# Softmax logits with the eight keys of a row innermost, in a two-layer-type network on one core

## The chip, the cores and the metric

The kernel runs on one core of a Trainium2 chip. A core has a matrix engine (TensorE, "PE" in the profile), a vector engine (VectorE, "DVE"), a scalar engine (ScalarE, "ACT"), a general engine (GpSimd, "POOL") and a queue that starts transfers (SyncE, "SP"). Each takes its own instructions in order and waits on semaphores for the others. The working memory, SBUF, and the memory that TensorE writes, PSUM, both have 128 partitions; a shape such as 128x1280 means 1280 numbers of float32 in each partition. The metric is the time of one execution on the device in microseconds; several executions are summarised by their median.

## The reference

A sequence of 2048 rows of 640 numbers passes through four layers, each added to its input after a normalisation of the rows: local attention, a Fourier mixing, local attention, the same mixing.

```python
def _A_ref(x, wqkv, wo):              # H = 32 heads of Dh = 20; W, dil = 8, 2
    q, k, v = (x @ wqkv) split by head
    idx = pos[:, None] - (arange(W) * dil)[None, :]      # 8 keys a row, every second row back
    logits = einsum("bhsd,bhswd->bhsw", q, kg) * scale   # kg, vg gathered by idx
    logits = where(idx >= 0, logits, -1e9)
    attn = softmax(logits, axis=-1)                      # over the 8 keys
    o = einsum("bhsw,bhswd->bhsd", attn, vg)
    return o.reshape(B, S, D) @ wo
def _B_ref(x, dft_seq_re, dft_seq_im, dft_hid_re, dft_hid_im):
    a, b = x @ dft_hid_re.T, x @ dft_hid_im.T
    return dft_seq_re @ a - dft_seq_im @ b
x = x + _A_ref(layernorm(x), wqkv, wo); x = x + _B_ref(layernorm(x), ...)
x = x + _A_ref(layernorm(x), wqkv, wo); x = x + _B_ref(layernorm(x), ...)
```

## The kernel before, in words

The rows are dealt to 4 chunks (`NC`) of 128 partitions with 4 rows each (`NJ`). The 32 heads are cut into 8 groups of 4 (`NE`, `HE`). One group of one chunk is a *unit* `u` of attention, 32 units in a layer; a unit is worked off in two halves (`jp`), each with two rows a partition: 2 rows x 8 keys x 4 heads x 20 = 1280 products. A half is a *step* `s = 2u + jp`; steps run from about -7 to 66. Functions are put into a plan by `at(step, phase, function)`, and the list `PHASES` sets the order of phases within a step. In the attention layers the order of all five engines is exactly this written order. In the mixing layers (`LayerB`) only TensorE's order is written; the other engines' instructions there are ordered by the compiler's planner.

For one unit the engines do this:

- SyncE loads windows of keys and values (`w_load`, L420) and the queries (`q_load`); ScalarE copies the queries into PSUM (`q_copy`, L407), in the phase `qc` late in the step ahead.
- VectorE multiplies the queries by the keys (`qk_mul`, L434, 1280 products into one of four tiles `pr`). GpSimd adds the second ten of a head's 20 products to the first ten (L437), so that `qk_red` on VectorE (L444) sums 10 numbers a logit. In the steps listed in `WHOLE` (one list for each attention layer) GpSimd is left out and VectorE sums all 20.
- The logits of a unit, `lg`, lie in SBUF as row, key, head: 128 numbers a partition. The softmax on VectorE has six parts (`soft`): the mask (L459, in chunks that hold the beginning of the sequence), the maximum over the keys (L461), its subtraction (L463), the sum (L465), the reciprocal (L467) and the product (L469), which writes the probabilities `pp` to PSUM. Between L463 and L465 ScalarE takes the exponential (L452). The maximum and the sum run over the keys, which lie 4 numbers apart, because the 4 heads are innermost.
- `av_mul` (L474) multiplies the probabilities, each repeated over 20 numbers, by the values, and `av_tree` on GpSimd adds the 8 keys in three additions (L493, L494, L495). The last half of a layer is summed on VectorE instead (L490).

Beside this TensorE computes the projections to queries, keys and values (L365, evacuated by ScalarE at L372), transposes (L330, and L338 for the low halves, with copies by ScalarE at L334 and L353), the output projection (L518, added to the row by VectorE at L162, with the row statistics by ScalarE at L167, L169 and GpSimd at L177) and, as fill towards the end of a layer, the first products of the mixing layer (L976, with splits at L910 and L963). ScalarE is in order too: the exponential and the copy of the queries stand in its queue among the evacuations that TensorE waits for. TensorE's float32 products are made of three passes over high and low halves.

The first attention layer runs from about 40 to 390 us of the span, the second from about 870 to 1260. The tile `pq` is one bank of PSUM: the queries `qp`, the probabilities `pp`, the maximum `mx`, the sum `sm` and the mask `mk`.

## Time and profile before

| | |
|---|---|
| median of the runs | 1773.27 us (1769.95 to 1776.17, 3 runs) |
| the profiled execution | 1771.33 us, of which the span on the engines is 1769.3 us |
| TensorE busy | 1736.0 us (98%) |
| VectorE busy | 1388.5 us (78%) |
| ScalarE busy | 810.8 us (46%) |
| GpSimd busy | 624.6 us (35%) |
| mean granted clock of TensorE | 0.995 |

The profile is one execution. Rows of groups give line, engine, operation, the tiles written and read, the shapes, the count, then the busy time, the mean duration in ns, and the idle time ahead of them with what ended it. Rows of waits give who waited, for whom, the time in total, how often and the longest. Rows of stretches give the window, its length, and busy time (with instruction count) of TensorE, its weight loads ("PEld"), VectorE, ScalarE and GpSimd, then the granted clock, the share of the transfer engines, and GB/s. Rows in order of time give start and duration in us; a bracket is the idle time just before and its releaser. TensorE's instructions overlap, so its busy time is the union of their spans, and short stalls may hide in it.

### The profile page before, as it was taken

What the parts mean: (1) busy time and instruction counts of PE and PEld (TensorE: products, weight loads), DVE (VectorE), ACT (ScalarE), POOL (GpSimd) and SP (SyncE); (2) the same over time, 40 slices, a digit from 0 to 9 for tenths busy, and PEclk for the clock granted to TensorE, in tenths of its full rate; (3) what the DMA queues carried; (4) which work ended last, traced back from release to release, by engine and by line L of the source; (5) the groups of instructions that cost most, each with busy time, mean ns of one, the idle gap of its engine ahead of it and who ended that gap; (6) DMA issues with size and microseconds to landing.
All of it is one profiled execution on the core that took longest, in us unless ns stands there. A gap on an engine that the chain in (4) does not pass through costs nothing.

```text
span 1769.3 us, 26448 instructions
## 1 busy us (share of the span) xinstructions
PE 1736.0 (98%) x8798; PEld 1505.9 (85%) x8798; DVE 1388.5 (78%) x2127; ACT 810.8 (46%) x1686; POOL 624.6 (35%) x587
## 2 busy tenths in 40 slices
PE   9999998989999999999999999999999999999999
PEld 6889897878888888888898889988788888888888
DVE  5999999977767767767548999999777676686673
ACT  4654544554445445445534344444434443443441
POOL 3899988850000000000028998899200000000000
PEclk9999999999999999999999999999999999999999
DMA  7996769858777787786657866698688767867761
GB/s 269 309 325 212 220 202 311 274 170 277 274 254 232 243 269 232 246 270 222 206 185 223 264 213 219 202 334 275 203 283 290 247 211 243 260 218 239 255 203 53
DMA packets 270760, 426.19 MB, mean 241 GB/s; under 512 B 22528, under 2 KB 149504, under 8 KB 270368
## 3 DMA queue, kind: packets, MB, share of 16 engines
q1 hardware_dynamic: 267424, 422.54, 72.3%
q10 hardware_dynamic: 3200, 1.97, 0.4%
q8 instruction: 70, 1.15, 0.3%
q14 instruction: 66, 0.54, 0.1%
HBM read 339.28 MB, written 85.14 MB: 240 GB/s over the span
## 4 chain that ended last, share of the span: by engine, by line
PE 59%; DVE 20%; DMA 9%; POOL 5%; issue 4%; ACT 3%; SPq 0%; DVEq 0%; ACTq 0%; POOLq 0%
PE aux L1058 13%; PE t L1147 11%; PE m L1147 11%; PE m L365 9%; PE pq L1147 5%; PE xt L1147 5%; DVE pr L434 4%; DVE pr L474 3%; DMA xc<-stg 3%; PE aux L518 3%; DVE lg L444 2%; POOL pr L493 2%; DMA win<-kvb 1%; POOL pr L437 1%; DVE stg L1111 1%
## 5 line engine op out<-in xcount | busy, mean ns | idle before, releaser
L365 PE MATMUL m<-r,s 128*128 128x480 f32 x1920 | 436.2, 381 | 2.7 <-ACT r L129 2.2
L365 PEld LDWEIGHTS m<-r,s 128*128 128x128 f32 x1920 | 355.4, 188 | 56.3 <-ACT r L129 2.7
L1058 PE MATMUL aux<-r2a,zo 128*128 128x320 f32 x768 | 226.5, 310 | 0.0
L1140 ACT CAST r<-win 128x512 fp32r<-128x512 f32 x246 | 150.5, 620 | 158.4 <-DVE win L1176 75.4
L493 POOL TENSOR_TENSOR pr<-pr 128x640 f32<-128x640 f32 x126 | 208.2, 1652 | 37.3 <-DVE pr L474 36.7
L1058 PE MATMUL aux<-pr,zo 128*128 128x320 f32 x704 | 208.3, 308 | 0.0
L177 POOL TENSOR_TENSOR stats<-stats,mhalf 128x1 f32<-128x1 f32 (+1 forms) x40 | 29.0, 726 | 493.8 <-ACT stats L173 484.7
L1141 DVE TENSOR_TENSOR r<-win,r 128x512 fp32r<-128x512 f32 x246 | 166.3, 688 | 45.0 <-ACT r L1140 43.8
L434 DVE TENSOR_TENSOR pr<-pq,win 128x1280 f32<-128x1280 f32 x128 | 189.7, 1483 | 9.7 <-ACT stg L372 4.8
L474 DVE TENSOR_TENSOR pr<-pq,win 128x1280 f32<-128x1280 f32 x128 | 190.7, 1491 | 4.9
L437 POOL TENSOR_TENSOR pr<-pr 128x640 f32<-128x640 f32 x118 | 168.8, 1431 | 16.2 <-DVE pr L434 15.7
L1147 PE MATMUL m<-r,r 128*128 128x512 f32 x594 | 152.6, 392 | 0.0
L1058 PEld LDWEIGHTS aux<-r2a,zo 128*128 128x128 f32 x768 | 144.1, 188 | 2.0
L1147 PE MATMUL t<-r,r 128*128 128x512 f32 x498 | 135.1, 393 | 1.7 <-PE t L1147 1.7
L1058 PEld LDWEIGHTS aux<-pr,zo 128*128 128x128 f32 x704 | 132.2, 188 | 2.1
L1147 PEld LDWEIGHTS m<-r,r 128*128 128x128 f32 x594 | 111.4, 188 | 24.7
L976 PE MATMUL m<-s,r 128*128 128x512 f32 x384 | 119.8, 400 | 4.0 <-DVE zo L1038 1.5
L976 PE MATMUL t<-s,r 128*128 128x512 f32 x384 | 118.2, 395 | 0.3 <-DVE ot L1033 0.3
L494 POOL TENSOR_TENSOR pr<-pr 128x320 f32<-128x320 f32 x126 | 111.8, 887 | 9.9
L444 DVE TENSOR_REDUCE lg<-pr 128x64 f32<-128x640 f32 (+1 forms) x128 | 110.5, 863 | 4.7 <-POOL pr L437 4.6
L1147 PEld LDWEIGHTS t<-r,r 128*128 128x128 f32 x498 | 93.4, 188 | 23.7 <-PE t L1147 2.5
L372 ACT COPY stg<-m 128x480 f32<-128x480 f32 x128 | 70.9, 554 | 69.5 <-PE m L365 50.2
(290 smaller groups left out, 3233.1 us busy)
## 6 DMA issues: line engine op xcount, KB each, us to landing
win<-cs_in SPq DMA_DIRECT2D x351, 256.0 KB, 4.3
r<-xc SPq DMA_DIRECT2D x240, 256.0 KB, 4.3
win<-kvb SPq DMA_DIRECT2D x96, 440.0 KB, 5.6
xa<-cs_in SPq DMA_DIRECT2D x121, 256.0 KB, 3.9
win<-kvb SPq DMA_DIRECT2D x64, 360.0 KB, 4.5
xc<-stg SPq DMA_DIRECT2D x40, 512.0 KB, 4.2
kvb<-stg SPq DMA_DIRECT2D x60, 320.0 KB, 5.3
s<-c0b SPq DMA_DIRECT2D x26, 512.0 KB, 6.1
```

The source lines that it names most:

```text
L365: nc.tensor.matmul(mt[g][:, : 3 * F], st[:, a, k], wq[q][:, b, k], start=n == 0, stop=n == 14)
L434: nc.vector.tensor_tensor(pr, q, wview(u, jp, 0, [[1, FE]]), op=ALU.mult)
L437: nc.gpsimd.tensor_tensor(pv[:, :, 0:10], pv[:, :, 0:10], pv[:, :, 10:20], op=ALU.add)
L444: nc.vector.tensor_reduce(lgs[u][:, 2 * jp : 2 * jp + 2].rearrange("p j w h -> p (j w h)"), prq.pop((u, jp)), axis=AX.X, op=ALU.add,)
L474: nc.vector.tensor_tensor(pr.rearrange("p j w (h d) -> p j w h d", d=DH), lgs[u][:, 2 * jp : 2 * jp + 2].unsqueeze(4).to_broadcast([P, 2, ...
L493: g.tensor_tensor(pr[:, :, 0:4], pr[:, :, 0:4], pr[:, :, 4:8], op=ALU.add)
L494: g.tensor_tensor(pr[:, :, 0:2], pr[:, :, 0:2], pr[:, :, 2:4], op=ALU.add)
L976: self.last = nc.tensor.matmul(self.z[t][k], self.xn[c][:, a, j, k * P : (k + 1) * P], self.ct[s][:, b], start=s == 0 and i == 0, stop=s = ...
L1058: self.last = nc.tensor.matmul(self.ym[e][:, :320], zt[(k, a, ri)][:, j2 * P : (j2 + 1) * P], w[:, e * 320 : (e + 1) * 320], start=(k, a, ...
L1140: nc.scalar.copy(hi, raw)
L1141: nc.vector.tensor_tensor(lo, raw, hi.bitcast(F32), op=ALU.subtract)
L1147: nc.tensor.matmul(bank, w(a, kb), hl[b], start=start and (a, b) == (0, 0), stop=stop and (a, b) == (1, 0),)
```

## The change

The logits `lg` and the probabilities `pp` are laid out as head, row, key, so that the 8 keys of a head and row are adjacent; the maxima and sums are laid out as head, row. The reduction of the query products (`qk_red`) reads its tile in the same order as before and writes each result to its new place; the value product (`av_mul`) reads the probabilities through a view that gives the old order. The maximum and the sum now reduce a contiguous run. The number of instructions and the elements of each stay the same there. Step 63, the last query product of a layer, joins both lists in `WHOLE`: GpSimd's addition L437 goes, and VectorE's L444 sums 1280 numbers instead of 640 in this step.

```diff
-WHOLE = ((43, 45, 47, 49, 51, 55, 57, 59), (51, 57))
+WHOLE = ((43, 45, 47, 49, 51, 55, 57, 59, 63), (51, 57, 63))
...
-            prq[(u, jp)] = pv
+            prq[(u, jp)] = pv.rearrange("p (a h) d -> p a h d", h=HE)
 
         def qk_red(u, jp):
             if jp == 0:
-                lgs[u] = T([P, NJ, W, HE], "lg", bufs=2)
+                lgs[u] = T([P, HE, NJ, W], "lg", bufs=2)
             nc.vector.tensor_reduce(
-                lgs[u][:, 2 * jp : 2 * jp + 2].rearrange("p j w h -> p (j w h)"),
+                lgs[u][:, :, 2 * jp : 2 * jp + 2].rearrange("p h j w -> p (j w) h"),
                 prq.pop((u, jp)),
...
             if part == 0 and (u // NE) % 2 == 0:
-                mw = bass.AP(tensor=mk.tensor, offset=mk.offset, ap=[mk.ap[0], [1, NJ], [1, W], [0, HE]])
+                mw = bass.AP(tensor=mk.tensor, offset=mk.offset, ap=[mk.ap[0], [0, HE], [1, NJ], [1, W]])
...
             if part == 1:
-                v.tensor_reduce(mx, lg.rearrange("p j w h -> p j h w"), axis=AX.X, op=ALU.max)
+                v.tensor_reduce(mx, lg, axis=AX.X, op=ALU.max)
             if part == 2:
-                v.tensor_tensor(lg, lg, mx.unsqueeze(2).to_broadcast([P, NJ, W, HE]), op=ALU.subtract)
+                v.tensor_tensor(lg, lg, mx.unsqueeze(3).to_broadcast([P, HE, NJ, W]), op=ALU.subtract)
             if part == 3:
-                v.tensor_reduce(sm, lg.rearrange("p j w h -> p j h w"), axis=AX.X, op=ALU.add)
+                v.tensor_reduce(sm, lg, axis=AX.X, op=ALU.add)
...
             if part == 5:
-                v.tensor_tensor(pp, lg, sm.unsqueeze(2).to_broadcast([P, NJ, W, HE]), op=ALU.mult)
+                v.tensor_tensor(pp, lg, sm.unsqueeze(3).to_broadcast([P, HE, NJ, W]), op=ALU.mult)
...
-                lgs[u][:, 2 * jp : 2 * jp + 2].unsqueeze(4).to_broadcast([P, 2, W, HE, DH]),
+                lgs[u][:, :, 2 * jp : 2 * jp + 2].rearrange("p h j w -> p j w h").unsqueeze(4).to_broadcast([P, 2, W, HE, DH]),
...
-        pp = pq[:, NJ * FE : NJ * FE + NJ * W * HE].rearrange("p (j w h) -> p j w h", j=NJ, w=W)
+        pp = pq[:, NJ * FE : NJ * FE + NJ * W * HE].rearrange("p (h j w) -> p h j w", j=NJ, w=W)
...
-        mx = pq[:, o : o + NJ * HE].rearrange("p (j h) -> p j h", j=NJ)
-        sm = pq[:, o + NJ * HE : o + 2 * NJ * HE].rearrange("p (j h) -> p j h", j=NJ)
+        mx = pq[:, o : o + NJ * HE].rearrange("p (h j) -> p h j", j=NJ)
+        sm = pq[:, o + NJ * HE : o + 2 * NJ * HE].rearrange("p (h j) -> p h j", j=NJ)
```

## The prediction

> **What bounds the kernel now.** I read the page's totals first, then busy time by stretch, then who waited for whom, then the chain of waits.
>
> ```profile
> span 1769.3 us, 26448 instructions
> PE 1736.0 (98%) x8798; PEld 1505.9 (85%) x8798; DVE 1388.5 (78%) x2127; ACT 810.8 (46%) x1686; POOL 624.6 (35%) x587
> ...
> DVE  5999999977767767767548999999777676686673
> ```
>
> TensorE is idle for 33.3 us of the span (1769.3 - 1736.0); nothing that this change touches can win more than that and what the clock loses around the gaps. The row of digits (tenths busy in 40 slices of 44 us) shows where VectorE is full: slices 2 to 8 and 23 to 28, the two attention layers. In these stretches (columns: length, then busy us of PE, PEld, DVE, ACT, POOL, then granted clock):
>
> ```profile
> 53.00:272.00 219.00, 218.03 (x1130) 193.21 (x1129) 211.26 (x292) 117.54 (x297) 202.89 (x189) 1.00 0.78 249
> 272.00:300.00 28.00, 21.51 (x107) 17.54 (x106) 27.25 (x38) 11.16 (x32) 22.04 (x23) 0.92 0.94 329
> 300.00:372.00 72.00, 66.88 (x353) 58.10 (x351) 66.78 (x98) 36.01 (x85) 65.36 (x60) 0.97 0.75 256
> 1072.00:1160.00 88.00, 88.00 (x481) 79.72 (x479) 82.25 (x123) 40.58 (x102) 76.96 (x72) 1.00 0.70 222
> 1160.00:1249.00 89.00, 82.94 (x434) 71.42 (x432) 83.63 (x121) 40.84 (x104) 81.88 (x76) 0.98 0.85 295
> ```
>
> TensorE's idle time inside attention lies at the ends of the layers: 6.5 us (28 - 21.51) and 5.1 us (72 - 66.88) in the first, 6.1 us (89 - 82.94) in the second. What ends it, and what ScalarE waits for from 53 to 350:
>
> ```profile
> PE aux L338 <- ACT s L334: 3.9, 1, 3.9
> PE aux L330 <- POOL zo L495: 2.8, 1, 2.8
> PE t L338 <- ACT r L334: 2.3, 1, 2.3
> PE pq L330 <- POOL zo L495: 1.7, 1, 1.7
> ...
> ACT lg L452 <- DVE lg L463: 74.8, 28, 6.2
> ACT pq L407 <- DVE pr L474: 27.4, 14, 4.7
> ACT stg L372 <- PE m L365: 6.5, 7, 1.5
> ```
>
> TensorE waits for copies by ScalarE and for GpSimd's trees; ScalarE, in order, waits 102 us for VectorE's subtract (L463) and value product (L474), and 6.5 us for TensorE. So late VectorE work reaches TensorE through ScalarE's queue. The chain of waits from 53 to 386 agrees:
>
> ```profile
> by line: DVE pr L434 15.8%; DVE pr L474 12.6%; issue 9.3%; DVE lg L444 7.5%; PE aux L518 7.1%; POOL pr L493 5.8%; POOL pr L437 4.2%; POOL pr L494 3.2%; DVE pq L461 2.4%; DVE pq L465 2.0%; DMA win<-kvb 1.9%; DMA xa<-x_in 1.7%; POOL zo L495 1
> ```
>
> **The change, part by part.** The durations (columns: times, busy us, mean ns):
>
> ```profile
> L474 DVE TENSOR_TENSOR pr<-pq,win 128x1280 f32<-128x1280 f32 x128 | 190.7, 1491 | 4.9
> L434 DVE TENSOR_TENSOR pr<-pq,win 128x1280 f32<-128x1280 f32 x128 | 189.7, 1483 | 9.7 <-ACT stg L372 4.8 <-ACT pq L407 4.1 <-DMA win<-kvb 0.7
> L444 DVE TENSOR_REDUCE lg<-pr 128x64 f32<-128x640 f32 x118 | 95.7, 811 | 4.7 <-POOL pr L437 4.6
> L465 DVE TENSOR_REDUCE pq<-lg 128x16 f32<-128x128 f32 x64 | 25.2, 394 | 8.1 <-ACT lg L452 2.0 <-ACT xa L194 0.5
> L461 DVE TENSOR_REDUCE pq<-lg 128x16 f32<-128x128 f32 x64 | 25.0, 391 | 2.1
> L469 DVE TENSOR_TENSOR pq<-lg,pq 128x128 f32<-128x128 f32 x64 | 18.9, 296 | 2.2
> L463 DVE TENSOR_TENSOR lg<-lg,pq 128x128 f32<-128x128 f32 x64 | 17.8, 278 | 0.1
> L444 DVE TENSOR_REDUCE lg<-pr 128x64 f32<-128x1280 f32 x10 | 14.8, 1476 | 0.0
> L490 DVE TENSOR_REDUCE zo<-pr 128x160 f32<-128x1280 f32 x2 | 4.7, 2360 | 0.1
> ```
>
> *The two softmax reductions (L461, L465).* They read four elements apart now and side by side afterwards. L444 reads along the row: (1476 - 811) / 640 = 1.04 ns an element and 146 ns fixed, with 64 results. 128 elements would cost 146 + 133 = 279 ns, yet they cost 391 and 394. L490, which also reads with a stride, costs 2360 for the 1280 elements that L444 reduces in 1476: 0.69 ns more an element; here it is (391 - 279) / 128 = 0.88. Number of results does not explain it, since L444 has 64 and no excess. After: 279, or 297 if writing to PSUM adds what L469 has over L463 (18 ns). I take 297, since these also write PSUM: 94 + 97 = 0.19 us a unit (32 units a layer); the other end is 0.23. I use 0.20.
>
> *Subtract, multiply by the reciprocal, mask (L463, L469, L459).* Their large operands stay contiguous and only the repeated small one turns; L474 reads a value repeated 20 times at (1491 - 1483) = 8 ns more than L434. I take 0, bounds -8 and +8 ns each, under 0.8 us a layer.
>
> *The query reduction (L444) now writes, and the value product (L474) now reads, 64 places 32 elements apart.* One hop per 10 or 20 elements. No row has this; the bound from above is a hop at L461's excess, 64 x 0.88 = 56 ns each, the bound from below is 0: there is nothing to gain, as both are contiguous now. I take 0, since 9 or 19 element times lie between hops and L490's and L461's price is for one at every element.
>
> [...]
>
> *Step 63 summed whole.* It removes GpSimd's L437 and adds 1476 - 811 = 665 ns to VectorE, once a layer, where both are late:
>
> ```profile
> 365.99 1.51 POOL L437 TENSOR_TENSOR pr<-pr 128x640 f32<-128x640 f32 x1
> 367.46 1.53 POOL L493 TENSOR_TENSOR pr<-pr 128x640 f32<-128x640 f32 x1
> 367.53 0.82 DVE L444 TENSOR_REDUCE lg<-pr 128x64 f32<-128x640 f32 x1 [1.32 <-POOL pr L437]
> 1236.63 1.43 POOL L437 TENSOR_TENSOR pr<-pr 128x640 f32<-128x640 f32 x1
> 1236.97 1.77 DVE L910 TENSOR_TENSOR r<-xa,r 128x640 fp32r<-128x640 f32 x1
> 1238.02 2.16 POOL L493 TENSOR_TENSOR pr<-pr 128x640 f32<-128x640 f32 x1
> 1238.67 0.81 DVE L444 TENSOR_REDUCE lg<-pr 128x64 f32<-128x640 f32 x1
> 1239.92 1.49 DVE L474 TENSOR_TENSOR pr<-pq,win 128x1280 f32<-128x1280 f32 x1
> 1241.71 2.13 POOL L493 TENSOR_TENSOR pr<-pr 128x640 f32<-128x640 f32 x1
> ```
>
> First layer: VectorE stood 1.32 us for L437; now it starts at once and is done 1.32 - 0.665 = 0.66 us earlier, and GpSimd's tree starts 1.47 us earlier. I take 0.7 (ends 0.66 and 1.47). Second layer: L444 follows VectorE's own L910 (1236.97 + 1.77), not GpSimd, so it ends 0.67 us later, and the value product, now over at 1241.41, at 1241.41 + 0.67 - 0.10 (L461) = 1241.98; GpSimd's tree, which started at 1241.71, then waits for it, 0.3 later. I take 0.3 lost; 0.67 is the worst, and a VectorE that comes earlier from before makes it 0.
>
> *What passes to TensorE.* First layer: a unit takes (372 - 53) / 32 = 10 us, so 22 lie ahead of 272: 22 x 0.20 = 4.4 us of VectorE. TensorE can follow only by its slack there. Back to back a product of L365 takes 25.98 / 120 = 0.217 us:
>
> ```profile
> 913.37 25.98 PE m L365 x120
> 892.53 8.79 PE aux L1058 x60
> 939.34 0.44 PE xt L330 x4
> 60.00:272.00 212.00, 211.03 (x1095) 187.11 (x1095) 204.37 (x284) 113.75 (x287) 197.85 (x184) 1.00 0.78 246
> L365 PE MATMUL m<-r,s 128*128 128x480 f32 x752 | 171.1, 381 | 0.0
> L518 PE MATMUL aux<-r2a,ot 128*128 128x320 f32 x208 | 32.8, 309 | 0.0
> ```
>
> From 60 to 272 that makes 752 x 0.217 = 162.8, 208 x 0.147 = 30.5 (L1058 streams 320 columns as L518 does), and for the other 1095 - 960 = 135, mostly transposes, 135 x 0.11 = 14.9: 208.2 of 212 us. The slack is between the idle 1.0 (212 - 211.03) and 3.8; I take 3.0, nearer the upper end, because the busy time of a pipelined TensorE counts short stalls as work. From 272 on 10 units remain; the last two belong to the tail costed with step 63: 8 x 0.20 = 1.6. With 0.7 for step 63 the first layer gains 5.3 us, inside the 11.6 us that TensorE idles from 272 to 372. Second layer: before 1072 the chain runs on TensorE, whose idle time there is 0, so nothing counts; from 1072 to 1249 17 units x 0.20 = 3.4, less 0.3, is 3.1 of 6.1 us idle. What is late next is GpSimd: 202.89 of 219 us busy now, of 216 afterwards, 94%, so it still has room. The clock regained after shorter gaps (0.92 and 0.97) I count as nothing; fully regained it is 28 x 0.08 + 72 x 0.03 = 4.4 us, which lowers the range.
>
> Sum: 5.3 + 3.1 = 8.4 us. Profiled execution 1771.3 - 8.4 = 1762.9. The median of the runs shown, 1773.27, is 1.9 above that execution, so the forecast for a median is 1764.9, rounded 1765. A change under 0.3% (5.3 us) can hardly be told from none here.
>
> **Rivals.**
> *TensorE is the bound until 272.* ScalarE's 6.5 us of waits for L365 and the lower end of the slack (1.0) speak for it; ScalarE's 102 us for VectorE against it. Then the ends alone gain: 1.6 + 0.7 in the first layer and in the second 9 units after 1160, 1.8 - 0.3: 3.8 us, 1769.
> *All of it passes, and the clock with it.* 32 x 0.23 + 1.5 in the first layer, 17 x 0.23 in the second, 4.4 of clock: 17 us, 1756. The 1.00 clock before 272 and GpSimd's 203 of 219 us busy speak against it.
> *The hops move rather than go* (no faster, or slower). The stride leaves two reductions of 128 reads and enters 2 x 64 writes and 2 x 64 reads a unit. At 0.88 ns a hop the 256 hops cost 0.225 us, all that is won: 1773, no change. Above 1.4 ns a hop (0.36 - 0.20 = 0.16 us a unit lost over 64 units, half of it passed on) it ends 5 us slower, 1778. L474, which changes value 64 times at no visible price, speaks against it.
> *The planner.* The layers between have VectorE, ScalarE and the transfers ordered by the compiler's planner from the whole program; another order there could cost as well as give. TensorE idles 33.3 - 6.5 - 5.1 - 6.1 = 15.6 us outside attention; twice that would end 15.6 - 8.4 = 7 us slower, 1780. From 13.7 us on it decides. That the planner runs over those layers only, and that TensorE's order there is written out, speaks against it.
>
> **How the numbers follow.** Forecast 0.48 (1760 to 1768), all passes 0.15, TensorE bound 0.20, hops 0.08, planner or another loss 0.09. Faster is the first two: 0.63. Slower is the planner and a part of the hops: 0.11. The rest, 0.26, is no change. The range runs from just below the full gain, 1755, to no gain with a little of the hops, 1776; about 0.14 is outside.
>
> **What would show it.** L461 and L465 near 280 to 297 ns; L444 still near 811 and 1476, x116 and x12; L474 near 1491. TensorE's waits on L334 of 3.9 and 2.3 us and on L495 of 2.8 and 1.7 us shrink. VectorE's busy time falls by 64 x 0.20 - 1.3 = 11.5 us, to 1377. I am wrong if L444 or L474 grow by tens of ns, if the gaps stay although VectorE is earlier (then ScalarE's transfers or GpSimd hold them), or if TensorE's waits between the attention layers move by more than 3 us.

## The result, and the profile after

The changed kernel takes 1769.83 us (median of 22 runs, 1763.73 to 1773.96) beside 1772.72 us for the kernel before (22 runs, 1767.5 to 1776.2). The ratio is 0.9983, with a 95% interval of 0.9975 to 0.9991: a gain of 3.0 us (1.6 to 4.4), where 8.4 were forecast. It lies inside the 0.3% that were called hardly distinguishable from no change. The profiled execution took 1771.43 us.

First the totals of the page and the row of VectorE's busy tenths:

```profile
span 1769.5 us, 26446 instructions
PE 1735.6 (98%) x8798; PEld 1505.1 (85%) x8798; DVE 1377.6 (78%) x2127; ACT 811.3 (46%) x1686; POOL 622.3 (35%) x585
...
DVE  5999999987867767767648999999777686677673
```

VectorE lost 10.9 us of busy time (1388.5 to 1377.6) and GpSimd its two additions. The span of this execution is nevertheless 1769.5 us, as before. The groups of instructions show that the edit itself did what it says (times, busy us, mean ns):

```profile
L474 DVE TENSOR_TENSOR pr<-pq,win 128x1280 f32<-128x1280 f32 x128 | 190.7, 1491 | 5.0
...
L444 DVE TENSOR_REDUCE lg<-pr 128x64 f32<-128x640 f32 x116 | 94.3, 813 | 6.5 <-POOL pr L437 6.4
...
L469 DVE TENSOR_TENSOR pq<-lg,pq 128x128 f32<-128x128 f32 x64 | 18.9, 296 | 2.2
L461 DVE TENSOR_REDUCE pq<-lg 128x16 f32<-128x128 f32 x64 | 18.9, 295 | 2.1
L465 DVE TENSOR_REDUCE pq<-lg 128x16 f32<-128x128 f32 x64 | 18.8, 294 | 8.4 <-ACT lg L452 2.3 <-ACT xa L194 0.5
L444 DVE TENSOR_REDUCE lg<-pr 128x64 f32<-128x1280 f32 x12 | 17.8, 1480 | 0.0
L463 DVE TENSOR_TENSOR lg<-lg,pq 128x128 f32<-128x128 f32 x64 | 17.7, 277 | 0.1
```

L461 and L465 fell from 391 and 394 ns to 295 and 294; nothing else in these rows moved by more than 4 ns. So the question is not what VectorE gained, but what reached TensorE. By stretches (length, then busy us of PE, PEld, DVE, ACT, POOL, then clock):

```profile
60.00:272.00 212.00, 211.46 (x1098) 187.79 (x1097) 202.27 (x286) 114.70 (x289) 199.15 (x184) 1.00 0.79 249
272.00:300.00 28.00, 22.69 (x112) 18.33 (x111) 27.25 (x38) 12.10 (x36) 22.68 (x23) 0.91 0.96 335
300.00:372.00 72.00, 67.86 (x358) 59.43 (x358) 67.46 (x100) 35.92 (x84) 65.51 (x61) 0.97 0.75 257
...
1160.00:1249.00 89.00, 83.92 (x439) 71.97 (x440) 80.66 (x120) 39.29 (x99) 78.54 (x74) 0.99 0.84 286
```

TensorE was busy 0.4, 1.2, 1.0 and 1.0 us longer in these stretches. The waits of TensorE from 272 to 390 us, and, in the second fence, of TensorE from 1160 to 1262 us (total, times, longest):

```profile
PE aux L338 <- ACT s L334: 4.5, 2, 3.8
PE aux L330 <- POOL zo L495: 1.8, 2, 1.2
```

```profile
PE pq L330 <- POOL zo L495: 1.9, 1, 1.9
PE t L338 <- ACT r L334: 1.1, 1, 1.1
...
PE m L976 <- DMA s<-c0b: 0.4, 1, 0.4
```

The 3.9 us wait for L334 near 293 us is still 3.8. The first layer's wait for GpSimd shrank (2.8 to 1.2), the second layer's did not (1.7 to 1.9). L338's wait in the second layer went from 2.3 to 1.1, and a wait for a transform slice (L954) is new. ScalarE's waits from 53 to 350 us:

```profile
ACT lg L452 <- DVE lg L463: 71.3, 28, 6.4
ACT pq L407 <- DVE pr L474: 24.3, 15, 4.6
ACT stg L372 <- PE m L365: 10.5, 13, 1.8
```

It waits 6.6 us less for VectorE (74.8 + 27.4 before) and 4.0 us more for TensorE (6.5 before).

### The profile page after: what moved, and what is told of

It is laid out like the page before. It is cut to its first block, busy times and chain, and to the rows that moved or that the text cites. A ratio compares the mean times of both kernels' runs of the same rounds, so it can differ in the third digit from the quotient of the medians.

```text
span 1769.5 us, 26446 instructions
## 1 busy us (share of the span) xinstructions
PE 1735.6 (98%) x8798; PEld 1505.1 (85%) x8798; DVE 1377.6 (78%) x2127; ACT 811.3 (46%) x1686; POOL 622.3 (35%) x585
## 4 chain that ended last, share of the span: by engine, by line
PE 72%; DVE 11%; DMA 8%; ACT 3%; issue 2%; POOL 2%; SPq 0%; ACTq 0%; DVEq 0%; POOLq 0%
PE m L365 18%; PE aux L1058 13%; PE t L1147 10%; PE m L1147 10%; PE aux L518 6%; PE pq L1147 5%; PE xt L1147 5%; DMA xc<-stg 3%; DVE pr L474 1%; DVE pr L434 1%; PE m L976 1%; PE t L976 1%; DMA xa<-wre_in 1%; DVE stg L1111 1%; POOL pr L493 1%
## 5 line engine op out<-in xcount | busy, mean ns | idle before, releaser
L493 POOL TENSOR_TENSOR pr<-pr 128x640 f32<-128x640 f32 x126 | 206.3, 1637 | 34.1 <-DVE pr L474 33.6
L177 POOL TENSOR_TENSOR stats<-stats,mhalf 128x1 f32<-128x1 f32 (+1 forms) x40 | 28.9, 722 | 497.7 <-ACT stats L173 488.5
L434 DVE TENSOR_TENSOR pr<-pq,win 128x1280 f32<-128x1280 f32 x128 | 189.7, 1482 | 12.5 <-ACT pq L407 7.3
L474 DVE TENSOR_TENSOR pr<-pq,win 128x1280 f32<-128x1280 f32 x128 | 190.7, 1491 | 5.0
L437 POOL TENSOR_TENSOR pr<-pr 128x640 f32<-128x640 f32 x116 | 167.0, 1440 | 15.8 <-DVE pr L434 10.7
L976 PE MATMUL m<-s,r 128*128 128x512 f32 x384 | 119.1, 397 | 5.8 <-DVE s L963 1.6
L976 PE MATMUL t<-s,r 128*128 128x512 f32 x384 | 118.3, 395 | 0.4 <-DVE ot L1033 0.3
L444 DVE TENSOR_REDUCE lg<-pr 128x64 f32<-128x640 f32 (+1 forms) x128 | 112.1, 876 | 6.5 <-POOL pr L437 6.4
L372 ACT COPY stg<-m 128x480 f32<-128x480 f32 x128 | 70.8, 554 | 78.6 <-PE m L365 58.3
```

The lines of the kernel that those rows point to most:

```text
L434: nc.vector.tensor_tensor(pr, q, wview(u, jp, 0, [[1, FE]]), op=ALU.mult)
L437: nc.gpsimd.tensor_tensor(pv[:, :, 0:10], pv[:, :, 0:10], pv[:, :, 10:20], op=ALU.add)
L444: nc.vector.tensor_reduce(lgs[u][:, :, 2 * jp : 2 * jp + 2].rearrange("p h j w -> p (j w) h"), prq.pop((u, jp)), axis=AX.X, op=ALU.add,)
L474: nc.vector.tensor_tensor(pr.rearrange("p j w (h d) -> p j w h d", d=DH), lgs[u][:, :, 2 * jp : 2 * jp + 2].rearrange("p h j w -> p j w h" ...
L493: g.tensor_tensor(pr[:, :, 0:4], pr[:, :, 0:4], pr[:, :, 4:8], op=ALU.add)
L976: self.last = nc.tensor.matmul(self.z[t][k], self.xn[c][:, a, j, k * P : (k + 1) * P], self.ct[s][:, b], start=s == 0 and i == 0, stop=s = ...
```

## How the traces are compared

One trace has a noise of its own, so I divide each at four marks: the eleventh evacuation of projections (L372), the last row addition (L162) of the first attention layer, the first evacuation of the second layer, and its last row addition. All are starts of single rows in order of time. The tail is the end of the second layer, between the 60th and the last of the program's 64 half-row additions (L162). These are all the traces of this study, us:

| kernel | first attention | first mixing | second attention | of it the tail |
|---|---|---|---|---|
| before, three traces | 335.2, 335.3, 334.7 | 487.1, 487.6, 489.7 | 383.8, 383.4, 383.1 | 26.4, 26.4, 27.9 |
| after, three traces | 331.5, 332.4, 332.5 | 489.0, 488.1, 487.4 | 383.4, 382.8, 382.8 | 28.5, 27.1, 28.3 |
| e1, layout alone | 330.5 | 491.5 | 382.4 | 27.7 |
| e2, step 63 alone | 335.5 | 489.9 | 386.5 | 29.0 |
| e4, step 63 in the first layer only | 331.2 | 487.9 | 383.5 | 26.3 |
| e7, e4 with the slice loaded earlier | 331.4 | 488.0 | 382.5 | 27.7 |
| e5, before with more VectorE work | 338.9 | 491.9 | 385.8 | 26.7 |
| e3, after without the maximum | 323.1 | 490.1 | 379.1 | 24.8 |
| e6, e1 without the maximum | 325.2 | 489.9 | 380.3 | 25.8 |
| e8, e3 with the slice loaded earlier | 323.9 | 491.2 | 379.0 | 24.8 |
| f2, before, one-operand split | 333.0 | 489.6 | 382.3 | 27.3 |
| f1, after, one-operand split | 328.9 | 487.7 | 382.7 | 25.7 |
| f3, e1, one-operand split | 330.1 | 486.4 | 380.7 | 25.5 |
| g2, f2 with the slice loaded earlier | 332.6 | 489.6 | 382.0 | 27.3 |
| g1, f1 with the slice loaded earlier | 332.2 | 488.1 | 379.3 | 25.8 |
| g3, f3 with the slice loaded earlier | 330.0 | 488.5 | 379.7 | 25.6 |

Means of three: the first attention layer gained 2.9 us (335.1 to 332.1; forecast 5.3), the second 0.4 (383.4 to 383.0; forecast 3.1). The rest of the program is the same code.

## The experiments

**The two parts by themselves.** e1 has the new layout with the old lists:

```diff
-WHOLE = ((43, 45, 47, 49, 51, 55, 57, 59, 63), (51, 57, 63))
+WHOLE = ((43, 45, 47, 49, 51, 55, 57, 59), (51, 57))
```

> The new layout with the old lists of whole steps (step 63 is again halved by GpSimd). Theory A (VectorE's lateness sets the ends of the attention layers, as forecast): the layout carries the gain, step 63 gives 0.7 us in the first layer and costs 0.3 in the second, so this kernel is within 1 us of the changed kernel. Theory B (step 63 on VectorE spoils the end of the second attention layer, where the trace of the changed kernel is 3.2 us early at 1234 and only 1.2 us early at 1252): this kernel is 1 to 2 us faster than the changed kernel, 4 to 5 us faster than before.

Measured: 1769.86 us, ratio 0.9978 (0.9968 to 0.9988), 3.9 us faster, between the two theories. e2 has the old layout with 63 in both lists (the reverse of the layout's lines of the diff, `WHOLE` as in the change).

> The old layout with step 63 summed whole. Theory A: 0.7 - 0.3 = 0.4 us faster than before, not to be told from nothing. Theory B: 1 to 2 us slower than before.

Measured: 1776.31 us, ratio 1.0015 (1.0001 to 1.0028), 2.7 us slower. The layout carries the gain, about half of the 8.0 us that the prediction gave it (3.0 + 1.6 + 3.4); step 63, which was to gain 0.4 us, costs (0.2 to 5.0 us in the old layout). e4 takes it out of the second layer only:

```diff
-WHOLE = ((43, 45, 47, 49, 51, 55, 57, 59, 63), (51, 57, 63))
+WHOLE = ((43, 45, 47, 49, 51, 55, 57, 59, 63), (51, 57))
```

> The new layout, step 63 summed whole in the first attention layer alone. By the forecast: 0.3 us faster than the changed kernel. By the theory that step 63 on VectorE spoils the end of an attention layer: about as fast as the layout alone if only the second layer suffers (3 to 5 us faster than before), between the layout alone and the changed kernel if both do.

Measured: 1768.29 us, 0.9976 (0.9966 to 0.9987). Its interval overlaps those of the changed kernel and of e1, so the times alone do not place the cost; the tail does, once the clock is taken into account (further down). e4's tail is 26.3 us, as in two traces of the kernel before; those of the changed kernel are 27.1 to 28.5.

**How much of VectorE's time reaches TensorE.** e3 takes away more of the same kind, e6 the same with the old lists, e5 adds work to the kernel before:

```diff
-            if part == 1:
-                v.tensor_reduce(mx, lg, axis=AX.X, op=ALU.max)
-            if part == 2:
-                v.tensor_tensor(lg, lg, mx.unsqueeze(3).to_broadcast([P, HE, NJ, W]), op=ALU.subtract)
```

> The changed kernel without the maximum over the keys and its subtraction (both are left out; the softmax is the same in exact arithmetic). VectorE has 295 + 277 = 572 ns less a unit, three times what the layout took away. Theory A: the time goes on falling with VectorE's work until TensorE's idle time in attention (17.7 us before) is used up: 12 to 17 us faster than before. Theory C (TensorE itself bounds attention, and what is won at its end is given back at the start of the mixing layer): at most 3 us more than the changed kernel won, 4 to 6 us faster than before, and TensorE arrives earlier at the end of attention by more than it arrives earlier 100 us later.

Measured: 1756.73 us, 0.9902 (0.9887 to 0.9918).

> The layout without the maximum and its subtraction (left out, the softmax is the same in exact arithmetic), with the old lists of whole steps. Theory B (step 63 on VectorE costs): 1 to 3 us faster than with step 63 whole, 17 to 19 us faster than before. Theory A: within 1 us of it.

Measured: 1759.13 us, 0.9923 (0.9910 to 0.9936).

```diff
             if part == 4:
+                v.reciprocal(mx, sm)
                 v.reciprocal(sm, sm)
```

> The kernel before with the reciprocal of each unit computed twice, the first into a place not used any more: 255 ns more of VectorE a unit, about what the layout saves, in the other direction. Theory A: slower by as much as forecast for the saving, 6 to 11 us, since VectorE is the later one already (32 x 0.255 = 8.2 us in the first layer, 17 x 0.255 = 4.3 in the second). Theory C: VectorE has room behind TensorE, so 0 to 4 us slower.

Measured: 1782.28 us, 1.0047 (1.0029 to 1.0065), 8.3 us slower for 64 x 0.257 = 16.4 us of VectorE. The new layout saves 64 x 0.196 = 12.5 us for its 3.9; e3 saves another 64 x (0.295 + 0.277) = 36.6 us for 14.4 more than the changed kernel (0.9983 - 0.9902). So 0.5 us of the end for a microsecond of VectorE upward, 0.3 and 0.4 downward. The stretches show it inside the first layer, of e5 first and of e3 in the second fence, and in the third ScalarE's wait in e3 from 53 to 350 us:

```profile
60.00:272.00 212.00, 209.06 (x1077) 183.93 (x1075) 205.12 (x298) 112.52 (x285) 193.64 (x181) 1.00 0.76 243
```

```profile
60.00:272.00 212.00, 212.00 (x1107) 188.58 (x1106) 195.21 (x248) 117.72 (x292) 202.04 (x188) 1.00 0.79 255
```

```profile
ACT stg L372 <- PE m L365: 47.7, 32, 2.6
```

In e3 TensorE shows no idle time until 272 us and ScalarE waits 47.7 us for its products; 6.5 us in the kernel before, 10.5 in the changed one. Up to here VectorE has saved 22 x 0.20 = 4.4 us in the changed kernel and 22 x 0.77 = 16.9 in e3, and has 22 x 0.257 = 5.7 us more to do in e5. How much of it has reached TensorE? The 64th evacuation, at about 274 us, comes 1.3 us earlier in the changed kernel than before (means of three traces, 222.7 against 224.0 us after the eleventh), 5.3 us earlier in e3 and 3.4 later in e5. That looks like shares of 0.30, 0.31 and 0.60. But an evacuation stands in ScalarE's queue. In the kernel before it starts 3.9 us after the product that it copies has ended, in e3 0.04 us after it. The rows of the last fifteen products of the projections and of their evacuation, before and, in the second fence, in e3:

```profile
266.93 3.43 PE L365 MATMUL m<-r,s 128*128 128x480 f32 x15
...
274.31 0.55 ACT L372 COPY stg<-m 128x480 f32<-128x480 f32 x1
```

```profile
265.71 3.42 PE L365 MATMUL m<-r,s 128*128 128x480 f32 x15
...
269.18 0.56 ACT L372 COPY stg<-m 128x480 f32<-128x480 f32 x1
```

TensorE works off the same products in the same order in all kernels of the table, so its own progress can be compared product by product. These fifteen start 216.8 us after the eleventh evacuation in the kernel before (266.93 - 50.17), 217.0 and 216.7 in b2 and b3, the same kernel; 215.9, 215.9 and 216.0 in three traces of the changed one, 215.3 in e3 and 220.2 in e5. So 0.9 us of the 4.4 reached TensorE, and 1.5 of the 16.9: nearly four times the saving gave less than twice the gain. e6 and e8, also without the maximum, stand at 215.4 and 215.3. TensorE had about 1.5 us of slack here, and the layout alone used more than half of it. Of work that is added, more arrives (3.4 of 5.7 us).

The second layer is tighter still. From its first evacuation to the three transposes (L330) ahead of L338's wait, at 1159.64 us in the kernel before, it takes 287.1 to 287.2 us in all six traces with the old layout and no added work, 286.8 to 286.9 in all thirteen with the new layout, those without the maximum among them, and 288.4 in e5. The layout gains 0.3 us there, and taking away more gains nothing. What attention gains beyond these points it gains near the end of each layer: in the first, 2.0 of its 2.9 us in the changed kernel and 10.5 of 12.0 in e3 come after these fifteen products have started. So theory C of the expectations holds up to there, and theory A behind it.

**The same kernels again.** b2 and b3 are the kernel before, a2 and a3 the changed kernel, without any edit.

> The kernel before once more, for a second trace of it. In the one trace so far the mixing layer (from the last addition of the first attention layer at 385.8 to the first evacuation of the second at 872.5) takes 486.7 us; in the traces of the changed kernel and of four variants it takes 1.9 to 4.7 us more, in the same order of instructions. If that is a loss that follows from arriving earlier, this trace shows 486 to 487 us again. If the first trace was a fast one by chance, it shows 489 to 491.

> The changed kernel once more, for a second trace. If what attention wins is given back in the mixing layer: end of the first attention layer 2 to 5 us before the kernel before, and the mixing layer 488 to 491 us. If its loss at the end of the second attention layer is real (3.1 us early at 1230, 1.1 early at 1257 in the first trace), this trace loses 1 to 2 us there again.

> The kernel before once more, a third trace of it. It is taken for the first mixing layer, from the last row addition of the first attention layer to the first evacuation of the second layer's projections: 487.1 and 487.6 us in the two traces of the kernel before, 487.9 to 491.9 in eight traces of the others, with the same order of instructions. If the early end of the first attention layer is given back there, this trace shows 487 to 488 again; if the difference is chance, it may show 489 or more. The whole: 1769 to 1775 us.

> The changed kernel once more, a third trace of it. The first mixing layer took 489.0 and 488.1 us in its two traces. If that layer gives back what the first attention layer gained, this trace shows 488 or more, with the first attention layer near 332 us; if it is chance, 487 is as likely. The wait of L976 for the third slice in the second attention layer: 0.4 and 2.1 us so far, here 0.4 to 2.1; the granted clock near 1250 us fell in one of the two traces, and L518 was slow in that one. The whole: 1764 to 1772 us.

Measured, single times: 1771.37 and 1770.82 us; 1767.81 and 1770.59. The first mixing layer took 489.7 us in b3 and 487.4 in a3, and the means of three traces are equal (488.1 us). So the longer mixing layers of some kernels are within what traces of one kernel differ by, and no loss shows there. b3 also shows the second layer's L338 wait, which the prediction counted as VectorE's to shorten, at 0.7 instead of 2.3 us with no change of the code, and a tail 1.5 us longer. Both are taken up below.

**The new wait for the transform slice.** In the second layer SyncE issues the load of the third slice (L954) behind a store (L535) that waits for a row. In a2 this costs TensorE 2.1 us; rows of SyncE's issues and of the waiting product, in order of time:

```profile
1155.50 0.32 SPq L954 DMA_DIRECT2D s<-c0b  x1
...
1159.90 0.58 SPq L535 DMA_DIRECT2D xs<-xa  x1
...
1160.57 0.70 SPq L954 DMA_DIRECT2D s<-c0b  x1
...
1168.09 0.73 PE L976 MATMUL m<-s,r 128*128 128x512 f32 x2 [2.08 <-DMA s<-c0b]
```

e7 is e4 with this load one step earlier:

```diff
-                at(min(t - 1, 48 + z) if z < 3 else t - 1, "dmac", handoff.c_get, z)
+                at(min(t - 1, (48, 49, 49)[z]) if z < 3 else t - 1, "dmac", handoff.c_get, z)
```

> The changed kernel with step 63 whole in the first attention layer only, and in the second attention layer the load of the third transform slice (L954, z = 2) one step earlier, so that SyncE issues it ahead of the store of the row (L535) that it stands behind now. Nothing is left out. Without this move TensorE's product L976 waited for that slice 2.1 us (issued at 1161.1 us, landed near 1168.7). Theory (in the second layer the new wait for the transform slice takes back what the softmax gives): issued near 1156.6, right behind the slice before it, the slice lands near 1164, about 2 us before TensorE needs it; the wait goes and the time falls by 1 to 2 us against the kernel without the move, to 1766.3 to 1767.3 us, some 5 to 6 us below the kernel before; the second layer, 383.5 us from its first projection to its last row, becomes 381.5 to 382.5. Rival (the wait is cover for the next one: TensorE would otherwise wait for ScalarE's copies, VectorE's splits or GpSimd's trees a few us later): the wait goes, and others between 1170 and 1250 us grow by as much; 1768.3 us, second layer 383.5. The move can also cost: the queries and windows behind the load in SyncE's queue leave 0.4 us later; then 1769.

Measured: 1767.72 us, 0.9964 (0.9949 to 0.9979), faster than e4 on the mean, with overlapping intervals. Both loads now leave ahead of the store, and no wait of L976 for a slice is left:

```profile
1157.27 2.52 SPq L954 DMA_DIRECT2D s<-c0b  x2
...
1163.17 0.33 SPq L535 DMA_DIRECT2D xs<-xa  x1
```

The second layer up to its tail fell from 357.2 to 354.8 us (383.5 - 26.3, 382.5 - 27.7), but 1.4 us of that came back in the tail (26.3 to 27.7), where the granted clock was 1.00 in e4 and 0.94 in e7. e8 does the same to e3.

> The changed kernel (step 63 whole in both layers) without the maximum and its subtraction, and with the load of the third transform slice one step earlier, as in the run above. What is left out: the softmax is computed without the shift by the row's maximum. Without the move this kernel took 1756.7 us and waited 0.9 us for the slice. Theory (the slice's load holds the second layer): the wait goes and 0.5 to 1 us with it, 1755.7 to 1756.2. Rival (another wait comes in its place): 1756.7, no change.

Measured: 1755.11 us, 0.9890 (0.9873 to 0.9908), within e3's interval.

**VectorE's waits for GpSimd.** L910 on VectorE subtracts two rows that both lie in SBUF. The prediction quoted one of 1.77 us without asking why; when GpSimd is idle it takes 0.81 to 0.83 (48 rows in ten traces). It meets GpSimd differently from run to run. One of them, at 1126 us in the kernel before and, in the second fence, at 1128 us in b3, the same kernel:

```profile
1125.84 1.58 POOL L493 TENSOR_TENSOR pr<-pr 128x640 f32<-128x640 f32 x1
...
1126.28 1.82 DVE L910 TENSOR_TENSOR r<-xa,r 128x640 fp32r<-128x640 f32 x1 [0.51 <-ACT r L906]
```

```profile
1126.46 1.45 POOL L437 TENSOR_TENSOR pr<-pr 128x640 f32<-128x640 f32 x1
...
1127.83 0.83 DVE L910 TENSOR_TENSOR r<-xa,r 128x640 fp32r<-128x640 f32 x1
...
1127.94 2.15 POOL L493 TENSOR_TENSOR pr<-pr 128x640 f32<-128x640 f32 x1
```

GpSimd's L493 ends at 1127.42, and L910, started at 1126.28, ends 0.68 us after it. Of the 97 L910 in the ten traces that met a GpSimd instruction with over 0.15 us left, 96 ended 0.66 to 0.69 us after its end. It goes the other way too: L493 takes 1.58 us alone (median of 1186) and 2.16 when it starts under an L910 (median of 74). In the second fence it ends 1.43 us after L910 does (1130.09 and 1128.66). So in these rows the later of the two waits until the earlier is done and then needs nearly all of its own time (0.68 us of 0.82, 1.43 of 1.58), and the profile books the wait as busy time. What makes them exclude each other no run shows.

Over a whole run L910's excess over 0.82 us sums to 7.8, 7.9 and 6.5 us in the traces of the kernel before and 5.8, 4.2 and 5.7 in those of the changed one. The 9.4 us in the expectation below wrongly include L580, another subtraction of two rows in SBUF, five times in the first layer: its excess sums to 1.2 to 1.3 us before, 2.5 to 2.6 afterwards. To take L910's excess away, f2, f1 and f3 replace VectorE's L910 by an instruction with one operand, in the kernel before, the changed one and e1:

```diff
-            (nc.vector if on_vector else nc.gpsimd).tensor_tensor(
-                self.xn[c][:, 1, j], self.xl[(c, j)], self.xn[c][:, 0, j].bitcast(F32), op=ALU.subtract
-            )
+            hi = self.xn[c][:, 0, j].bitcast(F32)
+            if on_vector:
+                nc.vector.tensor_reduce(self.xn[c][:, 1, j], hi.unsqueeze(2), axis=AX.X, op=ALU.max)
+            else:
+                nc.gpsimd.tensor_tensor(self.xn[c][:, 1, j], self.xl[(c, j)], hi, op=ALU.subtract)
```

> The kernel before, with VectorE's split L910 (two operands in SBUF, 815 ns when GpSimd is idle) replaced by a reduction over one element that copies the high half: the same 640 results, but one operand only. What is left out: the low half then holds the high half instead of the remainder, on the rows whose split VectorE makes. In every trace L910 ended 0.68 us after the GpSimd instruction that ran when it came, up to 2.2 us long; in the attention layers of the kernel before these excesses sum to 9.4 us. Theory (VectorE waits for GpSimd in instructions with two operands in SBUF, and where it meets GpSimd differs from run to run and from kernel to kernel): the instruction takes near 0.8 us everywhere, GpSimd's trees do not run over 1.6 us beside it, and the time falls by a third to a half of 9.4, 3 to 5 us, to 1768 to 1770. Rival (the length of L910 has to do with its place, or is memory traffic): it stays at 1.2 to 2.1 us in the same places and the time stays at 1772.

> The changed kernel with the same replacement of VectorE's split (left out: the low half, as there). If the gain of the change went into L910's waits for GpSimd, the distance between this kernel and the one before with the same replacement is larger than the 3.0 us between the originals: 5 to 8 us, and the second attention layer, which gained 0.4 us with the waits (383.4 to 383.0), gains 2 to 3 without. If TensorE's own rate or the transfers ate it, the distance stays 2 to 4 us, and the second layer's gain below 1 us.

> The new layout with the lists of step 63 as before, and the same replacement of VectorE's split (left out: the low half, as there). With the waits for GpSimd, step 63 summed whole cost the second layer's last four row additions 0.6 to 0.8 us, because the L910 behind it met GpSimd's L493 and took 2.22 instead of 0.9 us. Without those waits the theory expects the plain sum of the prediction: whole costs 0.67 us of VectorE in the second layer's tail and saves the wait of 1.3 us in the first, so this kernel is 0 to 0.7 us slower than the changed one with the same replacement. If step 63 costs for another reason, this kernel is 1 us faster.

Measured: f2 1766.86 us, 0.9978 (0.9969 to 0.9986); f1 1762.96, 0.9956 (0.9941 to 0.9970); f3 1763.08, 0.9948 (0.9936 to 0.9960). The groups with L910 on VectorE of the kernel before, and of f2, where the replacement stands at L912:

```profile
L910 DVE TENSOR_TENSOR r<-xa,r 128x640 fp32r<-128x640 f32 x6 | 8.9, 1487 | 1.0 <-ACT r L906 1.0
L910 DVE TENSOR_TENSOR r<-r,r 128x640 fp32r<-128x640 f32 x6 | 8.7, 1455 | 0.0
```

```profile
L493 POOL TENSOR_TENSOR pr<-pr 128x640 f32<-128x640 f32 x126 | 203.6, 1616 | 38.4 <-DVE pr L474 37.5
...
L912 DVE TENSOR_REDUCE r<-r 128x640 fp32r<-128x640 f32 x16 | 13.0, 814 | 1.9 <-ACT r L906 1.0 <-ACT r L924 0.9
```

On the mean 814 ns, where twelve of the sixteen took 1487 and 1455. So L910's waits for GpSimd are real and cost each kernel 4 to 5 us on the mean (3.9 in the kernel before, 4.8 in the changed one, 5.3 in e1). But the distance from before to changed is 3.9 us without them (0.9956 against 0.9978), 3.0 with them. The 5 to 8 us of the expectation did not come, and in the single traces of f2 and f1 the second layer gained nothing (382.3 and 382.7). L910's waits took about a microsecond of the missing gain on the mean; the intervals leave room for none, and for some 4 us. The changed kernel meets GpSimd even less in L910 than the kernel before, and more in L580.

**Both obstacles away.** g2, g1 and g3 are f2, f1 and f3 with the slice loaded earlier, by e7's edit.

> The kernel before with VectorE's split replaced by the one-operand reduction (left out: the low half of those rows, as above) and with the third transform slice loaded one step earlier, ahead of the row's store. Without the earlier load: 1766.9 us, second attention layer 382.3, TensorE waited 1.1 us for the slice. Theory (two obstacles in the second layer, VectorE's waits for GpSimd and the slice behind the store): the wait goes, 0.5 to 1 us faster, 1766, second layer 381.5. Rival (the copies by ScalarE that follow hold it): 1766.9, second layer 382.3.

> The changed kernel with the same replacement (left out as there) and the earlier load. Without the earlier load: 1763.0 us, second layer 382.7, wait for the slice 2.0 us. Theory: the wait goes and the second layer falls to 380.5 to 381, the time to 1761 to 1762; its distance to the kernel before with both edits is 4.5 to 5.5 us, of which the second layer has 1 to 1.5 instead of the 0.4 of the originals. Rival: the second layer stays at 382 to 383 and the time at 1763; then neither obstacle is what keeps the change from paying there.

> The new layout with the lists of step 63 as before, the same replacement (left out as there) and the earlier load. Without the earlier load: 1763.1 us, second layer 380.7, wait for the slice 1.7 us. Theory: second layer 379.5, the time 1761.5 to 1762. Against the changed kernel with both edits it tells again what step 63 costs in the second layer: 0.5 to 1 us if the summed step itself is the cost, nothing if only its meeting with GpSimd was.

Measured: g2 1768.21 us, 0.9969 (0.9957 to 0.9981); g1 1763.91, 0.9947 (0.9931 to 0.9962); g3 1764.17, 0.9946 (0.9934 to 0.9958). The load gives 0.9 thousandths in g2 and g1, 0.2 in g3, each within the intervals. The second layer falls from 382.0 to 379.3 us between g2 and g1, but 1.6 us of this is the tail, where the clock dropped in g2's trace (0.76 and 0.68 from 1246 to 1252 us) and not in g1's (1.00 from 1231 to 1267). Up to the tail it is 1.1 us (354.6 to 353.5, the second layer less the tail). These are single traces: from f2 to f1 the same part grew from 355.0 to 357.0, with waits of 1.1 and 2.0 us for the slice. The whole distance stays 3.9 us. So the forecast's 3.4 us for this part of the layer did not appear with these two obstacles away either. The way was not wholly free: L580 in the first layer still met GpSimd, for up to 2.22 us in f1 and g1.

## Why the prediction was right or wrong

**The cost of each instruction was right.** The two reductions came out at 295 and 294 ns (297 taken), a unit gained 0.196 us (0.20 taken), the products and subtractions stayed (277 and 296 ns), and VectorE's busy time came to 1377.6 us (1377 named). L444 went from 811 to 813 and from 1476 to 1480 ns, L474 stayed at 1491: the 64 hops, with 10 or 20 elements between them, cost next to nothing, as taken: 2 to 4 ns a reduction in L444 and none in L474.

**"What passes to TensorE" failed, in the slack that it gave TensorE.** The step let 3.0 of VectorE's 4.4 us pass before 272, from a slack between 1.0 and 3.8 us, and all of it in 272 to 372 and 1072 to 1249. On TensorE's own products 0.9 us had arrived by 267 us, and 1.5 when almost four times as much work was gone. So the slack was near the lower bound, TensorE's idle time, and the short stalls hidden in its busy time were worth half a microsecond and not 2.8. In the second layer the units from 1072 to 1160 were counted in full, although the prediction's own row has TensorE busy for 88.00 of 88 us there; by 1160 us 0.3 us had arrived, and no more without the maximum.

The ends came out closer. From the fifteen products to the end of the first layer the changed kernel gains 2.0 us (2.9 - 0.9) of the 2.3 that were forecast (8 x 0.20 and 0.7 for step 63). In the second layer three traces of each kernel give 1.4 us up to the tail (356.5 to 355.1 on the mean, the second layer less the tail) of 3.4, 1.1 of them behind 1160; but b3 is about 2 us shorter there than the other two traces of the same kernel, so this 1.1 us is not well established. The tail takes back 1.0 (26.9 to 27.9). Together that is 0.9 + 2.0 + 1.4 - 1.0 = 3.3 us in attention, where 8.4 were forecast.

ScalarE's wait for TensorE rose by 4.0 us where its waits for VectorE fell by 6.6; the prediction saw the 6.5 us that were there and gave the rival with TensorE as the bound until 272 a chance of 0.20. That rival named the right place, TensorE all but out of slack and the ends alone gaining, and nearly the right size (3.8 us). That its sum fits so well is in part luck, since it holds the same two terms for step 63, of which the gain did not show.

**The waits at the ends of the layers** were read as VectorE's. The 3.9 us for L334 at 293 us stays at 3.8 in the changed kernel; with the maximum gone, in e3, it falls to 1.3:

```profile
PE aux L338 <- ACT s L334: 2.0, 2, 1.3
```

The 2.3 us in the second layer is 2.3 in b2 and e2 too, but 0.7 in b3 without any change; with the new layout it is 0.6 or 1.1 (three traces of the changed kernel, e1, e4 and e7). So it shrinks by about a microsecond on the mean. In f2 and g2, with the old layout and the one-operand split, it is 0.6 and 1.3, which points to where L910 meets GpSimd as one reason; no run shows it instance by instance. With the new layout a wait for the slice often takes its place (2.1 us in a2 and e4, 0.9 in a3, none in e1), which the prediction had not listed as late next.

**Step 63 had the wrong sign.** The forecast was 0.7 gained and 0.3 lost. The second layer, rows in order of time, before (the first L910 stands in the prediction) and after:

```profile
1241.53 0.90 DVE L910 TENSOR_TENSOR r<-xa,r 128x640 fp32r<-128x640 f32 x1
...
1243.39 1.49 DVE L474 TENSOR_TENSOR pr<-pq,win 128x1280 f32<-128x1280 f32 x1
```

```profile
1233.64 0.81 DVE L910 TENSOR_TENSOR r<-xa,r 128x640 fp32r<-128x640 f32 x1
...
1234.37 1.48 DVE L444 TENSOR_REDUCE lg<-pr 128x64 f32<-128x1280 f32 x1
...
1236.21 1.49 DVE L474 TENSOR_TENSOR pr<-pq,win 128x1280 f32<-128x1280 f32 x1
...
1237.78 1.57 POOL L493 TENSOR_TENSOR pr<-pr 128x640 f32<-128x640 f32 x1 [0.33 <-DVE pr L474]
...
1237.82 2.22 DVE L910 TENSOR_TENSOR r<-xa,r 128x640 fp32r<-128x640 f32 x1
...
1240.96 1.49 DVE L474 TENSOR_TENSOR pr<-pq,win 128x1280 f32<-128x1280 f32 x1
```

With L437 gone the first L910 no longer waits for it (1.77 to 0.81 us), and the next comes 0.04 us after L493 and waits all of it through (0.90 to 2.22). From the first L910 to the last value product it takes 7.32 us (1240.96 - 1233.64) instead of 6.42 (1243.39 - 1236.97). The prediction had counted the 0.67 us of the longer sum and, of the quoted 1.77 us, only where it ended. Where the granted clock is 1.00 over the tail, the tail is 0.7 us longer with the step whole (27.1 in a2 against 26.3 in e4 and 26.4 before). Where the clock fell (0.94), it is 28.3 and 28.5 against 27.7 in e1 and e7 and, in the old layout, 29.0 in e2 against 27.9 in b3. With the one-operand split it is 0.2 longer (25.7 and 25.8 against 25.5 and 25.6), close to the 0.3 that the prediction gave; so the meeting with L493 makes up most of it. In the first layer e2 has an L910 of 2.19 us in that place as well, 0.82 before; its layer is 0.4 us longer than the mean of the three traces before, too little to tell, and the forecast gain of 0.7 us does not show. Where VectorE is far ahead the step seems to pay: e3 is 2.1 thousandths faster than e6, with intervals that overlap a little, and its tail is 1.0 us shorter.

**The planner** reordered nothing: the order of instructions on VectorE, ScalarE, SyncE and GpSimd is the same in both kernels, apart from the two additions that are gone.

What stays open: which meetings of the engines decide what arrives at the end of a layer, instance by instance; the 1 to 2 us by which single traces of one kernel differ in the first 50 us; and the second mixing layer. From the last row addition to the end it took 513.0, 511.2 and 511.0 us in the three traces before and 514.3, 512.4 and 514.2 in those of the changed kernel. That is 1.9 us more on the mean, all of it in the first 120 us. The other kernels took 511.5 to 513.6 us with the new layout and 511.7 to 512.3 with the old. Part of what attention won may be given back there; these traces do not settle it.

The fastest kernel here is e8 (1755.11 us). It leaves out the shift by the maximum, which is safe only where the logits are known to stay small.

## What to carry to other kernels

Here a saving on VectorE passed to TensorE only up to TensorE's slack (0.9 of 4.4 us and 1.5 of 16.9 by 267 us), and the slack was close to the idle time that the profile shows (1.0 us). Before trusting a larger estimate, measure it with a kernel that removes much more work and one that adds some. Compare the bounding engine's own instructions, one by one: a mark on another engine, such as an evacuation by ScalarE, moves with that engine's lateness (3.9 us behind its product before, 0.04 in e3). Ask of every instruction that takes longer than its shape says what the other engines were doing then; here a wait for GpSimd stood in the profile as VectorE's work (L910, 0.82 us alone and up to 2.22), and removing one GpSimd addition moved that wait rather than ended it (1.77 to 0.81 us, and 0.90 to 2.22 in the next L910). Take two or three traces of the same kernel before calling a wait of 2 us a property of it (2.3 us in the kernel before, 0.7 in b3).

## What the runs showed of the hardware

VectorE's L910, which has two operands in SBUF, and GpSimd's additions waited for each other's end, in both directions: L910 took 0.82 us alone and 2.22 behind a whole L493 (changed kernel), L493 1.58 alone and 2.16 behind an L910. L444, L474 and L912, VectorE's instructions with one operand in SBUF, kept their duration beside the same GpSimd work: in the kernel before L444 (640 numbers) took 0.80 to 0.83 us and L474, whose other operand is in PSUM, 1480 to 1493 ns; L912 took 814 ns on the mean in f2, and 0.81 or 0.82 us in eight rows of g3 beside a GpSimd instruction.

After the same short wait the granted clock fell in one run and not in another. The end of one and the same wait, in the kernel before and, in the second fence, in b3, with two stretches of b3 in the third:

```profile
1248.54 0.70 PE L330 MATMUL pq<-ident,zo 128*128 128x128 f32 x4 [1.71 <-POOL zo L495]
...
1249.70 2.17 PE L518 MATMUL aux<-r2a,zo 128*128 128x320 f32 x12 [0.46 <-ACT zo L334]
```

```profile
1248.46 0.70 PE L330 MATMUL pq<-ident,zo 128*128 128x128 f32 x4 [1.70 <-POOL zo L495]
...
1249.63 2.87 PE L518 MATMUL aux<-r2a,zo 128*128 128x320 f32 x12 [0.46 <-ACT zo L334]
```

```profile
1249.00:1252.00 3.00, 2.54 (x13) 2.23 (x12) 1.26 (x4) 0.65 (x2) 0.00 (x0) 0.80 0.00 0
1252.00:1255.00 3.00, 3.00 (x15) 3.00 (x15) 0.50 (x2) 1.42 (x5) 0.37 (x1) 0.63 0.28 109
```

Waits of 1.71 and 1.70 us end 0.08 us apart in the span; after one the granted clock stays at 1.00, after the other it is 0.80 and 0.63 in the next two stretches of 3 us, and the tail is 1.5 us longer (27.9 against 26.4). A drop is in the second layer's end also in two of three traces of the changed kernel and in e1, e2 and e7 (0.94 over the tail), in f2 (down to 0.50 in a stretch of 3 us) and in g2 (0.68). What decides it no run here shows.

L461, a reduction over 128 elements, took 295 ns with its keys adjacent and 391 with them four apart: 0.75 ns an element more with the stride.
